# Fifty extra matrix products of ones on TensorE during the weight decode of an attention and SoLU kernel

## The chip, the cores and the metric

The kernel runs on one core of a Trainium2 chip. The metric is the device time of one execution in microseconds; several executions of the same program are timed and their median is given. In the profile PE is TensorE, PEld its weight loads, DVE is VectorE, ACT is ScalarE, POOL is GpSimd and SP is SyncE, which issues most of the DMA transfers; a queue of an engine is written ACTq or SPq.

## What is computed

The reference does two things in a row. For 8 batches and 8 heads of 576 positions with 64 features it computes masked attention (heads 0 to 3 see the last 32 positions, heads 4 to 7 the earlier positions of the same residue modulo 32). The result, 4608 tokens of 512 features, then goes through a feed-forward part with two weight matrices:

```python
scores = np.where(masks, q @ k.T / sqrt(D), -1e9)
attn = softmax(scores); x = attn @ v            # (4608, 512)
h = x @ w_in                                    # w_in (512, 1024)
solu = h * softmax(h)
ln = (solu - mu) / np.sqrt(var + 1e-06) * g_ln
out = ln @ w_out                                # w_out (1024, 512)
```

## The kernel before

The inputs w_in and w_out lie in memory as 64-bit words (double precision), which no engine computes with. So the start of the kernel decodes them: four loads of 1 MB each for w_in (in `prep_w`) and four for w_out (in `prep_o`), issued by SyncE. For each load `decode` has two passes of ScalarE (L619, L620) and one of VectorE (L621) that turn the word into a single-precision number. Of the decoded weights `gram` (L314) forms products of each piece with itself on TensorE, whose diagonal VectorE sums (L318), and `pow2_scale` (L334 on TensorE, L338 and L341 on VectorE) makes a power of two from the sum, by which the weights are scaled. Then w_in is split into a 16-bit high part (L637, ScalarE) and a low part: for two of the four pieces on VectorE (L639), for the other two on TensorE (L647 and L648, with the matrix wdiag from L634) with a copy by ScalarE (L651). The products go to the PSUM tile h_ps, which has three banks. For w_out, L659 to L665 make the scale.

The attention runs beside it in units of up to 12 blocks: scores on TensorE (L439 adds the mask, L444 multiplies q and k, into s_ps), maximum and subtraction on VectorE (L450, L451), exponential on ScalarE (L452), sum and reciprocal on VectorE (L453, L457, L458), scaling on GpSimd (L461), the two 16-bit parts of the weights on ScalarE (L466) and, in the first batches, GpSimd (L468), a transposing DMA by SyncE (L472), the product with v on TensorE (L493, into x_ps), and the split of the result on ScalarE (L509) and VectorE (L510). L381 and L382 on VectorE combine the scales of v and w_in. When the tokens of a tile are there, the feed-forward part follows in 36 tiles of 128 tokens: 24 products with w_in (L551 to L553, into h_ps), row statistics on VectorE (L558 and later), and 24 products with w_out (L594 to L596).

No scheduler orders this. `Plan.add` numbers the steps in the order of the code and notes which step reads or writes what; the list ORDER, written out in the file, gives the sequence in which the steps are emitted, and each engine runs its own steps in that sequence and waits only on the steps it depends on. Steps 36 and following are those of `prep_w` behind the four decodes. The tile `ones` (128 by 128, 16-bit) is filled at the start by VectorE and serves as stationary matrix in L334.

Of the kernel before, what the change touches and what calls it, by code (L numbers as in the profile page):

```python
# [21 lines left out]
P = 128  # L22
# [28 lines left out]
WLO = (0, 1)  # L51


ORDER = [
# [45 lines left out]
]  # L100

BANKED = ("h", "x")
# [59 lines left out]
def attn_solu_kernel(ctx: ExitStack, tc: tile.TileContext, qloc, qstr, kloc, kstr, vloc, vstr, w_in, w_out, g, masks, out):  # L162
    nc = tc.nc
# [79 lines left out]
    add = plan.add  # L243
# [531 lines left out]
```

## Time and profile before

| | |
|---|---|
| median of 3 runs | 503.44 us (501.87 to 504.1) |
| the profiled execution | 503.95 us, span 502.2 us |
| busy: PE | 470.0 us (94%), 4834 products |
| busy: DVE, ACT, POOL | 353.5 us (70%), 292.7 us (58%), 159.6 us (32%) |
| mean granted TensorE clock | 0.979 |
| chain that ended last | PE 81%, DMA 7%, DVE 6%, issue 2%, ACT 2% |

The span is the time from the first to the last instruction of one profiled execution; the execution's own time is a little longer. Busy shares are averages over the whole span, and this kernel has a start of some 60 us, with loads and decoding, that is unlike the rest; so the table tells little about the start, and the views by stretch of time tell more. A busy time of PE counts a product from its start to its modelled end, so that the products of a dense row overlap in it: the distance from start to start is what a product costs there.

### The profile page before, as it was taken

To read this page: it belongs to the slowest core of one execution; us is meant where nothing else is said; L and a number is where in the kernel's file an instruction comes from. 1 tells how busy PE (TensorE), PEld (TensorE's weight loads), DVE (VectorE), ACT (ScalarE), POOL (GpSimd) and SP (SyncE) were. 2 spreads that over 40 slices of the span, in tenths; PEclk is the share of its full clock that TensorE was granted. 3 is DMA by queue.
4 is the path that set the end of the run, shared out by engine and by line. 5 is a ranking of instruction groups with operands and counts; after the bars stand their busy time and mean duration, and the time that the engine had idled before them with its cause. 6 is when DMAs were issued, how large, how long until landed. Compare 5 with 4: busy or idle time off the path is not lost.

```text
span 502.2 us, 11705 instructions
## 1 busy us (share of the span) xinstructions
PE 470.0 (94%) x4834; PEld 246.3 (49%) x4834; DVE 353.5 (70%) x636; ACT 292.7 (58%) x396; POOL 159.6 (32%) x256
## 2 busy tenths in 40 slices
PE   1468799999999999999999999999999999999997
PEld 1455454455445554455445554555445555544443
DVE  2789999688743897498856987488755997665430
ACT  1798886757546556554657365644647554554441
POOL 3324424723160334212331535312510435251120
PEclk9867999999999999999999999999999999999999
DMA  8999998577999499968994997998975789543272
GB/s 248 405 337 297 298 181 197 182 190 110 205 210 264 126 197 240 210 192 167 236 199 138 204 210 199 210 258 152 226 164 160 167 171 183 109 85 82 56 144 77
DMA packets 168102, 96.51 MB, mean 192 GB/s; under 512 B 137840, under 2 KB 154608, under 8 KB 167536
## 3 DMA queue, kind: packets, MB, share of 16 engines
q1 hardware_dynamic: 162432, 84.77, 76.6%
q10 hardware_dynamic: 5616, 10.98, 6.7%
q8 instruction: 38, 0.62, 0.5%
q14 instruction: 16, 0.13, 0.1%
HBM read 40.03 MB, written 9.44 MB: 98 GB/s over the span
## 4 chain that ended last, share of the span: by engine, by line
PE 81%; DMA 7%; DVE 6%; issue 2%; ACT 2%; SPq 1%; POOL 1%; ACTq 0%; DVEq 0%; POOLq 0%
PE h_ps L551 12%; PE h_ps L553 11%; PE h_ps L552 11%; PE o_ps L594 11%; PE o_ps L595 10%; PE o_ps L596 10%; PE x_ps L493 5%; PE s_ps L444 5%; DMA vtwo<-vstr 2%; DMA pt<-p 2%; DMA ct<-c 1%; PE s_ps L439 1%; DMA vrl<-vloc 1%; DVE st L558 1%; DVE obuf L621 1%
## 5 line engine op out<-in xcount | busy, mean ns | idle before, releaser
L461 POOL TENSOR_TENSOR t<-t,m 128x648 f32<-128x648 f32 (+4 forms) x34 | 51.8, 1526 | 201.8 <-DVE m L458 163.6
L551 PE MATMUL h_ps<-w,xhi 128*128 128x512 f16 x280 | 106.3, 380 | 0.8 <-DVE eu L572 0.8
L553 PE MATMUL h_ps<-w,xlo 128*128 128x512 f16 x280 | 106.1, 379 | 0.0
L552 PE MATMUL h_ps<-w,xhi 128*128 128x512 f16 x280 | 106.1, 379 | 0.0
L594 PE MATMUL o_ps<-obuf,ct 128*128 128x512 f16 x272 | 103.3, 380 | 0.5 <-DMA ct<-c 0.3
L596 PE MATMUL o_ps<-obuf,ct 128*128 128x512 f16 x272 | 103.1, 379 | 0.0
L595 PE MATMUL o_ps<-obuf,ct 128*128 128x512 f16 x272 | 103.1, 379 | 0.0
L558 DVE TENSOR_REDUCE st<-h_ps 128x1 f32<-128x1024 f32 x35 | 42.6, 1218 | 36.7 <-PE h_ps L553 36.5
L569 ACT ACTIVATE eu<-h_ps,st,vsc 128x1024 f32<-128x1024 f32 x31 | 37.2, 1201 | 35.8 <-DVE st L559 25.2
L576 ACT ACTIVATE c<-eu,st 128x1024 f16<-128x1024 f32 x36 | 41.2, 1144 | 23.0 <-DVE st L575 18.7
L577 DVE SCALAR_TENSOR_TENSOR c<-eu,st,c 128x1024 f16<-128x1024 f32 x36 | 45.7, 1273 | 11.7 <-ACT c L576 11.6
L572 DVE SCALAR_TENSOR_TENSOR eu<-h_ps,st,eu 128x1024 f32<-128x1024 f32 x35 | 44.7, 1277 | 11.7 <-ACT eu L569 10.8
L444 PE MATMUL s_ps<-k,q 64*54 64x54 f32 (+1 forms) x1280 | 40.5, 273 | 7.9 <-DMA k<-kloc 5.4
L452 ACT ACTIVATE t<-t 128x648 f32<-128x648 f32 (+4 forms) x34 | 26.1, 771 | 35.4 <-DVE t L451 35.0
L579 ACT ACTIVATE junk<-eu,st 128x1024 bf16<-128x1024 f32 x36 | 41.2, 1143 | 7.8 <-DVE st L575 4.7
L551 PEld LDWEIGHTS <-xhi 128*128 128x128 f16 x288 | 28.1, 98 | 35.3 <-issue 1.9
L596 PEld LDWEIGHTS <-ct 128*128 128x128 f16 x288 | 28.2, 98 | 34.0
L553 PEld LDWEIGHTS <-xlo 128*128 128x128 f16 x288 | 28.2, 98 | 34.0
L594 PEld LDWEIGHTS <-ct 128*128 128x128 f16 x288 | 28.1, 98 | 32.7 <-DMA ct<-c 0.7
L444 PEld LDWEIGHTS s_ps<-k,q 64*54 64x54 f32 (+1 forms) x1280 | 39.7, 199 | 8.4 <-DMA k<-kloc 5.6
L585 POOL TENSOR_SCALAR st<-st 128x1 f32<-128x1 f32 x36 | 19.4, 540 | 75.5 <-ACT junk L579 73.4
L552 PEld LDWEIGHTS <-xhi 128*128 128x128 f16 x288 | 28.2, 98 | 31.0
(156 smaller groups left out, 691.2 us busy)
## 6 DMA issues: line engine op xcount, KB each, us to landing
out<-ob ACTq DMA_DIRECT2D x36, 256.0 KB, 3.5
vtwo<-vstr SPq DMA_DIRECT2D x8, 768.0 KB, 7.8
vd<-vtwo SPq DMA_DIRECT2D x14, 384.0 KB, 5.4
vrl<-vloc SPq DMA_DIRECT2D x8, 640.0 KB, 5.2
k<-kstr SPq DMA_DIRECT2D x8, 594.0 KB, 5.4
q<-qloc SPq DMA_DIRECT2D x8, 576.0 KB, 5.7
k<-kloc SPq DMA_DIRECT2D x8, 576.0 KB, 5.4
q<-qstr SPq DMA_DIRECT2D x7, 594.0 KB, 7.4
```

The source lines that it names most:

```text
L444: nc.tensor.matmul(s_ps[row : row + nq, pair, i * nk : (i + 1) * nk], q_raw[half][hs, q0 : q0 + (nq - 1) * nqb + 1 : nqb], k_raw[half][hs, ...
L461: add("pool", lambda: nc.gpsimd.tensor_tensor(tv, tv, sm.unsqueeze(2).broadcast_to([P, nx, nk]), op=ALU.mult), r=TM, w=T)
L551: nc.tensor.matmul(hv[:, i], xhi[:, cc, tok], whi[:, cc, cols], start=(cc == 0), stop=False)
L552: nc.tensor.matmul(hv[:, i], xhi[:, cc, tok], wlo[:, cc, cols], start=False, stop=False)
L553: nc.tensor.matmul(hv[:, i], xlo[:, cc, tok], whi[:, cc, cols], start=False, stop=(cc == 3))
L558: add("dve", lambda: nc.vector.tensor_reduce(low, hv, axis=AX.XY, op=ALU.max, negate=True), r=HH, w=[(ST, "low")])
L572: add("dve", lambda: nc.vector.scalar_tensor_tensor(uv, hv, ia, ev, op0=ALU.mult, op1=ALU.mult, accum_out=us), r=[*HH, E, (ST, "ia")], w=[ ...
L576: add("act", lambda: nc.scalar.activation(c[:, 0], u, AF.Identity, bias=mean, scale=1.0), r=[U, (ST, "mean")], w=[(C, 0)])
L577: add("dve", lambda: nc.vector.scalar_tensor_tensor(c[:, 1], u, mean, c[:, 0], op0=ALU.add, op1=ALU.subtract), r=[U, (ST, "mean"), (C, 0)] ...
L594: nc.tensor.matmul(o, ct[:, cc, :], ohi[:, cc, :], start=(cc == 0), stop=False)
L595: nc.tensor.matmul(o, ct[:, cc, :], olo[:, cc, :], start=False, stop=False)
L596: nc.tensor.matmul(o, ct[:, 8 + cc, :], ohi[:, cc, :], start=False, stop=(cc == 7))
```

## The change

Fifty steps are added to `prep_w` behind the decodes. Each is one product on TensorE: the stationary matrix is `ones`, the moving one is `ones` too, repeated four times to 512 columns, and the result goes to the third bank of h_ps. Nothing reads it before the bank is written anew. In the list ORDER the new steps are 36 to 85, all later numbers grow by 50, and the fifty are put in at eight places. Apart from that the sequence is the old one, and the programs of VectorE, ScalarE, GpSimd and SyncE are the same. The places, in the order of time on TensorE: two behind the L314 products of v and ahead of the first L334; eighteen behind that L334; thirteen behind the L314 products of the first piece of w_in; one between those of the third and the fourth piece; four behind the fourth; two between the L334 of w_in and that of v; two behind the latter; eight ahead of the unit whose masks are added at 39.33 us. The diff, with the list cut to one line:

```diff
 WLO = (0, 1)
+WARM = 50
...
-    12, 1, 2, 11, 9, 10, 15, 14, 16, 20, 3, 17, 24, 7, 18, 0, 13, 4, 8, 28, 5, 32, 70, 71, 72, 83, 73, 74, 84, 75, 85, 76, 59, 86, 77, 78, 60, 79, 21, 61, 87,
+    12, 1, 2, 11, 9, 10, 15, 14, 16, 20, 3, 17, 24, 7, 18, 0, 13, 4, 8, 28, 5, 32, 120, 121, 122, 133, 123, 124, 134, 125, 135, 126, 109, 136, 127, 128, 110,
+    129, 21, 111, 137, 36, 37, 112, 113, 114, 22, 138, 139, 146, 23, 118, 147, 116, 38, 39, 40, 41, 42, 43, 44, 45, 46, 47, 48, 49, 50, 51, 52, 53, 54, 55,
...
             decode(stage[cc], w_in[cc * P : (cc + 1) * P].rearrange("p (c f t) -> p c f t", c=2, t=2), ST[cc], ROOMS[cc], cc)
 
+        def idle():
+            nc.tensor.matmul(h_ps[:, 2], ones, ones.unsqueeze(1).broadcast_to([P, 4, P]), start=True, stop=True)
+
+        for _ in range(WARM):
+            add("pe", idle, r=["ones"], w=[("h", 2)])
         gram(w_sc[:, 4:5], [(flat[cc], ST[cc]) for cc in range(4)], "wm", (h_ps[:, 0, 0:P], ("h", 0)), (ob_sb[1][:, 0 : P // 2].bitcast(BF16), ("ob", 1)))
```

In the rows below, a line number of the changed kernel is 3 larger than that of the kernel before up to the new code, and 8 larger behind it; L636 is the new product. A row names the operation, the tile it writes, the tiles it reads and the shape.

On TensorE, before, the two L334 products (the scales of w_in and of v) are followed by the masks of the next unit:

```order
L334 LDWEIGHTS ones_110
L334 MATMUL h_ps<-w_sc_115,ones_110 128x1
L334 LDWEIGHTS ones_110
L334 MATMUL s_ps<-vs_78,ones_110 128x1
L439 LDWEIGHTS unit_85
L439 MATMUL s_ps<-mk_loc_83,unit_85 64x288
```

In the changed kernel, at the same place:

```order
L337 LDWEIGHTS ones_110
L337 MATMUL h_ps<-w_sc_115,ones_110 128x1
L636 LDWEIGHTS ones_110
L636 MATMUL h_ps<-ones_110 128x512
L636 LDWEIGHTS ones_110
L636 MATMUL h_ps<-ones_110 128x512
L337 LDWEIGHTS ones_110
L337 MATMUL s_ps<-vs_78,ones_110 128x1
```

Two of the new products now stand between the two scales (and two more behind the second).

On TensorE, before, the scores of one unit (k and q of the near positions, x12 instructions in a row) are followed at once by the masks of the unit that starts at 39.33 us:

```order
L439 LDWEIGHTS unit_85
L439 MATMUL s_ps<-mk_loc_83,unit_85 64x288
L444 MATMUL s_ps<-k_65,q_63 64x96 x12
L439 LDWEIGHTS unit_85
L439 MATMUL s_ps<-mk_str_84,unit_85 64x324
```

In the changed kernel the new products follow those scores:

```order
L442 LDWEIGHTS unit_85
L442 MATMUL s_ps<-mk_loc_83,unit_85 64x288
L447 MATMUL s_ps<-k_65,q_63 64x96 x12
L636 LDWEIGHTS ones_110
L636 MATMUL h_ps<-ones_110 128x512
```

Eight such pairs stand there before the masks follow.

## Rows read from the trace of the kernel before

**Rows 1.** The page's second part: the span in 40 equal slices of 12.56 us; each digit is a busy share in tenths, PEclk the granted TensorE clock in tenths.
```profile
PE   1468799999999999999999999999999999999997
...
PEclk9867999999999999999999999999999999999999
```

**Rows 2.** The windows view: the stretch (us from the span's start) and its length, then the busy time, with the number of instructions, of PE, PEld, DVE, ACT and POOL, then the granted clock, the DMA share and GB/s. The first four cover the two stretches at the lower clock, the one between them, and the time from the chain's last VectorE link to the end; the last is VectorE's run up to that link.
```profile
20.70:34.40 13.70, 7.88 (x132) 6.66 (x132) 13.19 (x14) 13.17 (x15) 2.36 (x3) 0.50 1.10 363
34.40:37.80 3.40, 1.32 (x30) 1.03 (x31) 2.41 (x12) 3.40 (x6) 1.74 (x6) 1.00 1.00 351
37.80:44.60 6.80, 5.27 (x94) 3.27 (x95) 6.28 (x15) 5.79 (x7) 2.81 (x3) 0.50 1.17 258
62.40:502.20 439.80, 433.14 (x4231) 219.85 (x4230) 306.89 (x548) 247.94 (x344) 136.97 (x214) 1.00 0.81 174
45.60:62.30 16.70, 14.00 (x209) 8.62 (x208) 16.23 (x29) 15.11 (x20) 7.10 (x6) 1.00 1.09 322
```

**Rows 3.** The chain of waits in order of time, three of its pieces between 57 and 63 us: start, length, engine and line.
```profile
60.50 0.18 DVE m L457
...
61.11 1.23 DVE o_sc L665
...
62.39 0.16 PE o_ps L334
```

**Rows 4.** The timeline of PE between 18 and 45 us: start, busy time, line, operation, and in brackets the idle time before it and what ended that.
```profile
18.30 0.16 PE L334 MATMUL o_ps<-vm,ones 128*128 128x1 bf16 x1 [0.47 <-DVE junk L318]
...
24.13 1.25 PE L444 MATMUL s_ps<-k,q 64*64 64x96 f32 x24 [5.42 <-DMA k<-kloc]
...
28.26 0.45 PE L439 MATMUL s_ps<-mk_loc,unit 64*64 64x288 bf16 x4 [1.91 <-DVE t L451]
...
32.00 1.92 PE L314 MATMUL h_ps<-ct 128*128 128x128 bf16 x16
34.83 0.18 PE L334 MATMUL h_ps<-w_sc,ones 128*128 128x1 bf16 x1 [0.91 <-DVE ob L318]
...
36.41 0.32 PE L439 MATMUL s_ps<-mk_loc,unit 64*64 64x288 bf16 x4 [0.34 <-DVE vsc L338]
36.53 0.86 PE L444 MATMUL s_ps<-k,q 64*64 64x96 f32 x24
39.33 0.49 PE L439 MATMUL s_ps<-mk_str,unit 64*64 64x324 bf16 x4 [1.94 <-DVE vsc L341]
...
40.96 0.27 PE L659 MATMUL o_ps<-unit,gm 128*1 128x128 bf16 x1
41.16 2.08 PE L647 MATMUL h_ps<-c,wdiag 128*128 128x512 f32 x2
...
43.59 1.24 PE L493 MATMUL x_ps<-pt,vd 118*64 118x54 f16 x40
```

**Rows 5.** The timeline of PE later, at the granted clock 1.00: the same products as some of group 4, and two products of 512 columns in a row.
```profile
45.93 1.02 PE L647 MATMUL h_ps<-c,wdiag 128*128 128x512 f32 x2
...
47.10 0.28 PE L493 MATMUL x_ps<-pt,ve 96*64 96x64 f16 x6
...
71.98 0.94 PE L493 MATMUL x_ps<-pt,vd 118*64 118x54 f16 x48
...
104.81 0.33 PE L439 MATMUL s_ps<-mk_str,unit 64*64 64x324 bf16 x4
...
106.26 0.39 PE L594 MATMUL o_ps<-obuf,ct 128*128 128x512 f16 x1
106.49 0.38 PE L595 MATMUL o_ps<-obuf,ct 128*128 128x512 f16 x1
```

**Rows 6.** The timeline of DVE between 33 and 58 us.
```profile
33.05 0.72 DVE L450 TENSOR_REDUCE m<-s_ps 128x6 f32<-128x576 f32 x1
...
41.26 0.28 DVE L660 TENSOR_REDUCE gm<-o_ps 1x1 f32<-1x128 f32 x1 [0.35 <-PE o_ps L659]
...
45.58 0.72 DVE L510 TENSOR_TENSOR xlo<-x_ps,xhi 128x540 f16<-128x540 f32 x1 [0.16 <-ACT xhi L509]
...
48.06 0.28 DVE L382 TENSOR_SCALAR vsc<-consts,vsc,w_sc 128x2 f32<-128x2 f32 x1
...
49.88 0.45 DVE L457 TENSOR_SCALAR m<-m 128x12 f32<-128x12 f32 x1
...
51.70 1.11 DVE L382 TENSOR_SCALAR vsc<-consts,vsc,w_sc 128x2 f32<-128x2 f32 x1
...
57.78 1.23 DVE L621 SCALAR_TENSOR_TENSOR obuf<-obuf,eu 128x1024 int32<-128x1024 int32 x1
```

**Rows 7.** The timeline of ACT between 43 and 57 us.
```profile
43.70 0.59 ACT L651 CAST w<-h_ps 128x512 f16<-128x512 f32 x1 [0.69 <-PE h_ps L648]
44.94 0.61 ACT L509 CAST xhi<-x_ps 128x540 f16<-128x540 f32 x1 [0.66 <-PE x_ps L493]
...
55.28 1.16 ACT L619 ACTIVATE obuf<-eu 128x1024 f32<-128x1024 f32 x1 [0.16 <-DMA eu<-w_out]
56.34 1.24 ACT L620 ACTIVATE eu<-eu,consts 128x1024 int32<-128x1024 uint32 x1
```

**Rows 8.** The timeline of POOL between 49 and 53 us.
```profile
49.01 1.29 POOL L468 TENSOR_TENSOR p<-t,p 128x576 f16<-128x576 f32 x1 [3.00 <-ACT p L466]
50.67 2.12 POOL L461 TENSOR_TENSOR t<-t,m 128x648 f32<-128x648 f32 x1 [0.37 <-DVE m L458]
```

89 rows, old and new, of the table ORDER are left out of this document.

## The prediction

> **What bounds the kernel now.** I read the 40 slices of the page first. TensorE is filled from about the fifth slice on and has holes before; its granted clock is below full only in the slices ahead of that [rows 1]. The stretches show where: the clock stands at 0.50, which is 1.2 GHz, from about 20.8 to 34.4 us and from 37.8 to 44.6 us, and at 1.00, 2.4 GHz, between them and for all the rest [rows 2]. From 62.4 us to the end TensorE is busy 433.14 of 439.80 us at 1.00: there it is the bound, nothing of its clock is left to win, and whatever ends the first 62 us sooner moves the end by as much. So the whole question is what sets the 62.4 us.
>
> The chain of waits answers it: the last link before TensorE's unbroken work is VectorE's L665 at 61.11, on which TensorE's L334 at 62.39 waits [rows 3]. Behind it VectorE has been at work almost without a stop: 16.23 of the 16.70 us from 45.6 to 62.3, while in the first cold stretch it was busy 13.19 of 13.70 us and ScalarE 13.17 [rows 2]. TensorE was busy 7.88 us there. The start is thus paced by VectorE and ScalarE and, behind them, by the loads; TensorE's low clock counts only where one of those two stands still for it. The reader should look for such places, and there are four: VectorE idles 0.35 us before L660 at 41.26 and 0.16 us before L510 at 45.58 (this one through ScalarE) [rows 6]; ScalarE idles 0.69 us before L651 at 43.70 and 0.66 us before L509 at 44.94 [rows 7]. All four lie at the end of the second cold stretch.
>
> **The fifty products.** Each has 512 columns and 128 rows; at 1.00 two like it start 0.23 us apart (106.26, 106.49) [rows 5]. At 0.50 I price one by the 16 products of 128 columns that take 1.92 us at 32.00: four of them are 0.48 us [rows 4]. They have no inputs to wait for, and every other engine's program is unchanged, so they cost only where TensorE comes late to its next real product. Gap by gap, at 1.00:
> Two stand ahead of L334 at 18.30, which had 0.47 us of waiting: 0.46 us, covered. Eighteen follow: 4.1 us from 18.46, to 22.6, and the masks behind them; the next real product waits for a load until 24.13 after 5.42 us of idleness. Covered, with about 1 us over.
> Thirteen stand ahead of L439 at 28.26, whose wait was 1.91 us: they need 3.0 us. But the neighbours shrink if the clock holds: the 24 products of L444 from 1.25 to 0.86 us (24.13 against 36.53), the eight of L314 by a quarter of 1.92, that is 0.48. The wait then has 2.8 us, TensorE is 0.2 late, and the scores from there are first read by VectorE at 33.05 [rows 4, 6]: covered.
> One and four stand within and behind L314 at 32.00, 1.15 us; the wait before L334 at 34.83 was 0.91 and the 16 products give back up to 0.96. Four lie between 35.01 and 36.41: 0.92 us in 1.40, less 0.16 for the L334 between them. Covered, within 0.1 to 0.2 us.
> Eight stand ahead of L439 at 39.33: 1.84 us in a wait of 1.94. This is the tightest place: cover 0.1 us. At 0.50 they take 3.84, and TensorE is late by 1.9 [rows 4].
>
> **What the clock gives back.** Before the clock fell at about 20.8 and 37.8 TensorE had been mostly idle (1.32 us of work in the 3.40 us to 37.8), and it rose at 44.6 after a stretch in which TensorE had 5.27 us of work in 6.80 [rows 2]. With the products in the waits it has work through nearly all of 17.8 to 45 us, so I take it to stay at 1.00 from 37.8 to 44.6. Then:
> VectorE. L439 and L444 at 39.33 take 1.63 us to L659; the same two take 1.45 at 104.81 to 106.26. L659 takes 0.27, and half of it is 0.13. L660 comes 0.18 to 0.31 sooner of its 0.35 [rows 4 to 6]. The 0.16 at 45.58 goes too. Together 0.34 to 0.47; I take 0.4. No clock can give VectorE more than the whole 0.51.
> ScalarE. From L647 to the start of L493 takes 2.43 us (41.16 to 43.59) and 1.17 at 1.00 (45.93 to 47.10); forty products of L493 take 1.24 and at 1.00 40/48 of 0.94, 0.78 [rows 4, 5]. TensorE then ends this work more than 1.6 us sooner, and both waits of ScalarE go: 1.35 us.
>
> **Where that goes.** ScalarE's gain ends at 55.28: there it already waits 0.16 us for the last load of the output weights [rows 7]. That load stands in SyncE's queue behind transposes which by the program follow ScalarE and GpSimd, and ScalarE first waits for TensorE at 43.70; so I take its landing as fixed. ScalarE's second decode step ends at 56.34 + 1.24 = 57.58 as before, and VectorE's L621, which reads it, started at 57.78 [rows 6]. So VectorE may come to this place as early as it likes; it gains at most 0.20 us beyond it. The cover of TensorE's low clock is this load and these two engines.
> Something can also be lost on the way. L382 on VectorE takes 0.28 us at 48.06 but 1.11 at 51.70, where it ends at 52.81, just when GpSimd's L461 (50.67 + 2.12 = 52.79) does: it stood still for it [rows 6, 8]. GpSimd's L468 at 49.01 waits for ScalarE; 1.35 sooner is 47.66, and the first L382, 0.4 sooner, is at 47.66 too. If it falls behind L468 it loses 0.83. In return L457 at 49.88 is free of L468, 0.45 to 0.18 [rows 3, 6], 0.27 back. So VectorE arrives at L621 between 0.4 + 0.27 = 0.67 early, cut to 0.20 by the load, and 0.4 - 0.83 + 0.27 = -0.16, late. I take a gain of 0.1, nearer the early end, since L382 is caught only if L468 starts first, and the two start together.
>
> **The sum.** The profiled execution took 503.95 us, the median of the three runs is 503.44, 0.51 below. 503.95 - 0.1 = 503.85 for a like execution, 503.3 for the median. Within 0.5% (2.5 us) counts as no change, about what a measurement of this kernel can tell; the runs of the one kernel before spread from 501.87 to 504.10.
>
> **The rivals.**
> (a) The products do not hold the clock: it falls as before. Where they stay covered the time is that of before, 503.4. For it: TensorE still idles from about 22.9 to 24.1.
> (b) The load is no fixed end, or lands sooner. Then VectorE's own count holds, 0.51 of idle time and the 0.27 of L457, 0.8 us at most: 502.6. Against it: the 0.16 us idle before 55.28 ends with that load.
> (c) Slower: the eight products ahead of L439 at 39.33 run at 0.50. They end 1.9 us late, L659 and with it VectorE's L660 come 1.9 later, and VectorE, with next to no idle time from there to 62.3, passes it to the end: 505.2. It decides from the point at which they take longer than 1.94 us, 0.24 each. For it: in the trace the clock fell at 37.8, in just this place. Against it: eight more products stand in the 4 us ahead.
> (d) TensorE's cold work paces the start after all, in one place or another of the two stretches at 0.50. It is 7.88 + 5.27 = 13.15 us [rows 2]; the full clock gives back half of it, 6.6 us: 496.8. Against it: VectorE was busy 13.19 of the 13.70 us of the first stretch, and of TensorE's gain only the four idle places above can pass on.
> The Trainium skill (TensorE: Matmul & The Clock Gate, Terms) goes further than (d): it puts the penalty of a throttled clock at the throttled time times one minus the clock's share. By the page's rule, as an estimate, the 20.5 us of the two stretches would be worth some 10 us, an end near 493. The trace does not bear it out, since in those stretches TensorE itself had only 13.15 us of work.
>
> **How the numbers follow.** Forecast 0.55; (a) 0.13; (b) 0.14; (c) 0.12; (d) 0.03; 0.03 for what I do not see, such as several groups running at 0.50 and pushing the 33.05 reader. The range reaches from (b) with the spread of the runs, 501.9, to (c), 505.3. Forecast, (a), (b) and (c) all lie within 2.5 us of before: same 0.86, with the tails of (b) and (d) faster 0.07, the tails of (c) slower 0.07.
>
> **What would show it.** Right: granted clock 1.00 through 20.8 to 45 us, L647 at about 41 in half its time, no idle time before L651 and L509, more idle time on ScalarE before the last load of the output weights, and L665 ending within a few tenths of 62.3. Wrong: L439 at 39.33 late, a landing of that load at another time, or a difference that arises after 62.4, where I expect a plain shift.

## The result, and the profile after

The changed kernel takes 507.15 us (median of 20 runs, 503.97 to 510.43) beside 503.45 us (20 runs, 501.39 to 506.65) of the kernel before on the same chip. The ratio is 1.0074, with a 95% interval of 1.0052 to 1.0096: 3.7 us slower. The prediction, 503.3 us with no change, was wrong, and the time lies above its range.

The profiled execution of the changed kernel is one of its quicker ones, 504.28 us with a span of 502.6 us. It shows most of what was forecast and, beside it, two things that were not. The windows view first (columns as in [rows 2], the first three and the last being the stretches shown there, the fourth a new one):

```profile
20.70:34.40 13.70, 11.22 (x164) 6.82 (x163) 13.19 (x15) 12.42 (x13) 2.62 (x3) 1.00 1.09 356
34.40:37.80 3.40, 1.53 (x26) 0.71 (x27) 1.18 (x6) 2.85 (x5) 1.19 (x5) 1.00 1.03 375
37.80:44.60 6.80, 6.58 (x125) 4.15 (x118) 6.49 (x15) 6.80 (x8) 2.81 (x3) 1.00 1.28 217
62.60:66.10 3.50, 3.42 (x10) 1.19 (x10) 3.26 (x10) 2.05 (x3) 1.06 (x2) 0.51 1.27 146
62.40:502.60 440.20, 434.64 (x4231) 220.33 (x4230) 307.15 (x549) 247.97 (x344) 137.24 (x215) 1.00 0.81 174
```

The clock stands at 1.00 through both stretches that were at 0.50. VectorE was busy 13.19 us of the first before and is so now: it gained nothing there. In the second stretch it is busy 1.18 us where it was 2.41. And there is a new stretch at 0.50, from 62.60 to 66.10 us, in TensorE's unbroken work.

The timeline of PE (columns as in [rows 4]):

```profile
22.26 0.32 PE L442 MATMUL s_ps<-mk_loc,unit 64*64 64x288 bf16 x4
...
27.95 0.32 PE L442 MATMUL s_ps<-mk_loc,unit 64*64 64x288 bf16 x4
...
36.76 0.16 PE L337 MATMUL s_ps<-vs,ones 128*128 128x1 bf16 x1 [1.87 <-DVE w_sc L341]
...
38.22 1.90 PE L636 MATMUL h_ps<-ones 128*128 128x512 bf16 x8
40.19 0.33 PE L442 MATMUL s_ps<-mk_str,unit 64*64 64x324 bf16 x4
...
41.69 0.22 PE L667 MATMUL o_ps<-unit,gm 128*1 128x128 bf16 x1
41.84 1.12 PE L655 MATMUL h_ps<-c,wdiag 128*128 128x512 f32 x2
```

The scale of v (36.76) was at 35.90 before: it comes 0.86 us late, behind a wait of 1.87 us. The eight products take 1.90 us, and the masks behind them stand at 40.19, not 39.33. The timelines of ACT and of DVE say why the scale is late. First the rows of before, of PE and of ACT:

```profile
35.90 0.16 PE L334 MATMUL s_ps<-vs,ones 128*128 128x1 bf16 x1 [0.90 <-DVE vs L327]
...
34.09 1.48 ACT L375 ACTIVATE junk<-vtwo 128x1536 bf16<-128x1536 f32 x1
```

Then those of the changed kernel, of ACT and of DVE:

```profile
34.95 1.48 ACT L378 ACTIVATE junk<-vtwo 128x1536 bf16<-128x1536 f32 x1 [1.47 <-DMA vtwo<-vstr]
...
43.77 0.56 ACT L659 CAST w<-h_ps 128x512 f16<-128x512 f32 x1
44.26 0.61 ACT L512 CAST xhi<-x_ps 128x540 f16<-128x540 f32 x1
...
55.59 1.15 ACT L622 ACTIVATE obuf<-eu 128x1024 f32<-128x1024 f32 x1 [0.24 <-DMA eu<-w_out]
```

```profile
36.55 0.16 DVE L330 TENSOR_REDUCE vs<-vm 128x1 bf16<-128x2 f32 x1 [2.35 <-ACT junk L378]
...
41.95 0.28 DVE L668 TENSOR_REDUCE gm<-o_ps 1x1 f32<-1x128 f32 x1 [0.17 <-PE o_ps L667]
...
48.50 1.12 DVE L385 TENSOR_SCALAR vsc<-consts,vsc,w_sc 128x2 f32<-128x2 f32 x1
...
61.74 0.88 DVE L673 TENSOR_TENSOR o_sc<-gm 128x1 f32<-128x1 f32 x1
```

TensorE is not the cause. ScalarE squares a part of the second batch's v (L378, the tile vtwo) and waits 1.47 us for its load, where before it came to these squares without a wait, just after the load had landed (34.04 us); VectorE (L330, then L341) waits 2.35 us for ScalarE; TensorE waits for VectorE. ScalarE's two waits of [rows 7] before L659 and L512 are gone, and it waits 0.24 us before 55.59. The chain of waits (start, length, engine and tile) names the load, and behind 62.68 the products at half clock:

```profile
26.47 8.40 DMA vtwo<-vstr
...
62.68 0.16 PE o_ps L337
62.84 0.45 PE h_ps L554
...
66.24 0.22 PE h_ps L556
```

The load was issued at 26.47 us. Before, it was issued at 27.04 and took 7.0 us; now it comes sooner, takes 8.4 and lands 0.8 us later. The DMA view of before at the load's issue:

```profile
vtwo<-vstr SPq DMA_DIRECT2D x1, 768.0 KB, 7.0
```

The DMA view of the changed kernel (queue, packets, MB, share of 16 engines; then an issue with its KB and us to landing), of 31 to 34.9 us and of the load's issue:

```profile
q8 instruction: 1, 0.02, 1.8%
...
vtwo<-vstr SPq DMA_DIRECT2D x1, 768.0 KB, 8.4
```

Between 31 and 34.9 us one packet of 16 KB goes through the queue that the view names instruction; 1.8% of 16 engines for 3.9 us are 1.1 us on one. In this execution all this costs little: the product that waits for o_sc is at 62.68, not 62.39 [rows 3], 0.29 later. From there the new stretch at 0.50 gives TensorE 1.50 us more busy time (434.64 against 433.14, [rows 2]); less idle time in the rest takes up most of it, and the span grows by 0.4 us in all. The median execution loses 3.7, so the rest had to be looked for in other executions: each lists its mean granted clock, and of the 20 the three quickest stand at 0.997 to 0.998 (504.0 to 505.1 us), two at 0.996 (505.7 and 506.0), the others at 0.989 to 0.993 (506.6 to 510.4).

### The profile page after: what moved, and what is told of

Read it like the earlier page. It is cut to its first block, busy times and chain, and to the rows that moved or that the text cites. A ratio compares the mean times of both kernels' runs of the same rounds, so it can differ in the third digit from the quotient of the medians.

```text
span 502.6 us, 11805 instructions
## 1 busy us (share of the span) xinstructions
PE 478.6 (95%) x4884; PEld 248.6 (49%) x4884; DVE 353.3 (70%) x636; ACT 292.7 (58%) x396; POOL 159.9 (32%) x256
## 4 chain that ended last, share of the span: by engine, by line
PE 84%; DVE 8%; DMA 4%; issue 2%; ACT 1%; POOL 0%; ACTq 0%; DVEq 0%; POOLq 0%
PE h_ps L554 12%; PE h_ps L555 12%; PE o_ps L597 12%; PE h_ps L556 12%; PE o_ps L599 11%; PE o_ps L598 11%; PE s_ps L447 6%; PE x_ps L496 5%; DMA vtwo<-vstr 4%; PE s_ps L442 2%; DVE obuf L624 1%; PE o_ps L317 1%; DVE st L561 1%; PE s_ps L599 1%; DVE vd L397 1%
## 5 line engine op out<-in xcount | busy, mean ns | idle before, releaser
L455 ACT ACTIVATE t<-t 128x648 f32<-128x648 f32 (+4 forms) x34 | 26.1, 770 | 35.3 <-DVE t L454 34.9
L599 PEld LDWEIGHTS <-ct 128*128 128x128 f16 x288 | 28.2, 98 | 34.0
L597 PEld LDWEIGHTS <-ct 128*128 128x128 f16 x288 | 28.1, 98 | 32.2
L598 PEld LDWEIGHTS <-ct 128*128 128x128 f16 x288 | 28.2, 98 | 31.1
```

The source lines that it names most:

```text
L597: nc.tensor.matmul(o, ct[:, cc, :], ohi[:, cc, :], start=(cc == 0), stop=False)
L598: nc.tensor.matmul(o, ct[:, cc, :], olo[:, cc, :], start=False, stop=False)
L599: nc.tensor.matmul(o, ct[:, 8 + cc, :], ohi[:, cc, :], start=False, stop=(cc == 7))
```

## The experiments

In every kernel below each product of the reference's computation is still there; only products that nobody reads come and go. The fifty stay at their eight places unless said. The kernel before was timed along with each set on the same chip: 503.64, 503.22, 502.97 and 503.14 us for the four sets in their order below. A loss in us is the ratio less one, times 503; the distance of two medians can differ from it by some tenths, and for the second sample of the changed kernel by 1.1 us (2.5 by the ratio, 3.6 by the medians).

**Is it the clock alone?** The first theory was that the clock falls in TensorE's last waits ahead of 62 us. Four kernels ran together. The changed kernel and the kernel before, unchanged, are a second sample of each:

> The changed kernel once more, unaltered, for the granted clock of each execution beside its time. T1 (the clock falls in TensorE's last waits ahead of its unbroken work, so that the first products there run at 0.50; the first profile showed it from 62.6 to 66.1 us): the mean granted clock differs between executions and the span follows it, about 1.7 us more for each 0.0034 of mean clock; a second profile shows a stretch at 0.50 near or behind 62 us, and none or little of it elsewhere. T2 (no clock in it: the fifty products come late to the real ones, and VectorE hands the lateness on): span and mean clock are unrelated, and L337 behind o_sc starts 3 us or more after the 62.4 us of the kernel before. T3 (the clock falls somewhere in the dense part behind 70 us): the stretch at 0.50 is there.

> The kernel before, unaltered, as the counterpart: all three theories give ratio 1.000 within its interval. T1: a mean clock of about 0.979 in most executions, which is the 20 us at 0.50 in the first 45 us, and seldom less; a stretch at 0.50 near 62 us is rare here. If falls near 62 us are as frequent here as in the changed kernel, T1 does not explain the difference.

The other two put eleven more products into the last two waits:

```diff
+        def fill():
+            nc.tensor.matmul(h_ps[:, 2], ones, ones.unsqueeze(1).broadcast_to([P, 4, P]), start=True, stop=True)
+        for _ in range(11):
+            add("pe", fill, r=["ones"], w=[("h", 2)])
```

In the list five stand ahead of the products x_ps of one unit and six ahead of the L337 product of o_sc, once in the changed kernel and once in the kernel before.

> The changed kernel with eleven more products of ones: five in TensorE's wait of 1.25 us ahead of the x_ps products at 57.06, six in the wait of 1.44 us ahead of the o_sc product at 62.68. T1: the clock no longer falls there, the mean clock is 0.998 or more in nearly all executions, and the time is 3 to 4 us below the changed kernel, 502.5 to 504. T2: the eleven cost what they are late, time 507 or a little above. T3: as the changed kernel, 507.

> The kernel before with the same eleven products in the same two waits and none of the fifty. T1: if the kernel before sometimes loses the clock there too, the time falls by up to 1 us and the spread shrinks to the lower end, 501.5 to 503; the mean clock stays 0.979 for the first 45 us. T2 and T3: no change, 503.4.

Measured: the changed kernel again 507.27 us, ratio 1.0050 (1.0019 to 1.0080); the kernel before again 503.07, 0.9992 (0.9972 to 1.0012); the changed one filled 506.46, 1.0052 (1.0027 to 1.0077); the one before filled 504.77, 1.0026 (0.9998 to 1.0054).

The second sample shows the clock's part. Its four executions at a mean clock of 0.999 to 1.000 took 502.6 to 504.1 us, as the kernel before; seven at 0.990 to 0.993 took 507.0 to 509.7. Its profiled execution is of the latter kind. Windows view, then the timeline of PE:

```profile
38.20:41.60 3.40, 3.40 (x20) 1.12 (x12) 3.30 (x8) 3.40 (x4) 1.38 (x2) 0.50 1.20 183
65.50:68.90 3.40, 3.40 (x10) 1.17 (x10) 3.16 (x9) 2.06 (x3) 0.00 (x0) 0.50 1.14 242
```

```profile
36.92 0.16 PE L337 MATMUL s_ps<-vs,ones 128*128 128x1 bf16 x1 [1.81 <-DVE vs L330]
...
38.46 3.45 PE L636 MATMUL h_ps<-ones 128*128 128x512 bf16 x8
41.84 0.33 PE L442 MATMUL s_ps<-mk_str,unit 64*64 64x324 bf16 x4
...
43.28 0.22 PE L667 MATMUL o_ps<-unit,gm 128*1 128x128 bf16 x1
...
65.47 0.16 PE L337 MATMUL o_ps<-o_sc,ones 128*128 128x1 bf16 x1 [2.58 <-DVE o_sc L673]
```

Here the clock falls behind the wait of 1.81 us, exactly onto the eight: 3.45 us in place of 1.90. L667 comes at 43.28, 1.59 us later than in the execution above and 2.32 later than before; o_sc's product comes at 65.47, 3.08 later than before. VectorE adds to it on the way: from the last L624 to L673 it takes 4.36 us where it took 3.33, and one L460 of 1.21 us in place of 0.17 makes that difference.

But the clock in the last waits is not the main cause. The filled kernel kept a mean clock of 0.996 to 1.000 in ten of its 12 executions and was as slow as the second sample of the changed one; in its profile the clock fell elsewhere, once at the very place where the load is late and once far behind, from 217.5 us:

```profile
36.60:40.00 3.40, 3.01 (x33) 1.53 (x33) 2.61 (x9) 3.40 (x7) 2.25 (x5) 0.50 1.58 354
217.50:220.90 3.40, 3.15 (x42) 2.10 (x42) 2.46 (x7) 2.32 (x3) 0.00 (x0) 0.50 0.06 23
```

Such a late fall does not need the fifty products: the profile of the kernel before, run again, has one from 212.9 to 216.3 us.

The filled kernel before settles nothing; its interval reaches to no change. So the load came under suspicion. The DMA view of the kernel before, run again (of 32.7 to 35 us, and of the load's issue):

```profile
q8 instruction: 1, 0.02, 2.9%
...
vtwo<-vstr SPq DMA_DIRECT2D x1, 768.0 KB, 7.0
```

Its load was issued at 25.71 and took 7.0 us, to 32.7; the packet came at 33.2, after it.

**Is it the instruction packet?** The theory now: TensorE's program has 100 more instructions (each product loads its stationary matrix first), so the packet that fetches the next block is asked for earlier and falls into the load. Four kernels ran together. The first has the fifty with one row and one column, which add the instructions but hardly any work:

```diff
-            nc.tensor.matmul(h_ps[:, 2], ones, ones.unsqueeze(1).broadcast_to([P, 4, P]), start=True, stop=True)
+            nc.tensor.matmul(h_ps[0:1, 2, 0:1], ones[:, 0:1], ones[:, 0:1], start=True, stop=True)
```

The second has only the last sixteen, with 4, 2, 2 and 8 at the last four of the eight places:

```diff
-        for _ in range(WARM):
+        for _ in range(16):
```

The third has 94 such tiny products (`short`) ahead of all others of TensorE. They are 188 instructions, and with the 68 of the first four places 256, 16 KB, ahead of the place where the packet is asked for:

```diff
-        for _ in range(WARM):
-            add("pe", idle, r=["ones"], w=[("h", 2)])
+        for i in range(144):
+            add("pe", short if i < 94 else idle, r=["ones"], w=[("h", 2)])
```

The fourth fills the wait for the scale of v, with nine full products ahead of it in place of two:

```diff
-        for _ in range(WARM):
+        for _ in range(57):
```

> The fifty products at their places, but each with one column and one row of the array in use, so that TensorE's program is as long as in the changed kernel (7232 rows) and the work and the clock are nearly those of before. T5 (code loading: TensorE's longer program brings a 16 KB packet of the instruction queue, which is at 34.3, 33.2 and 34.0 us in the three profiles without the fifty, to 31.8 to 32.0 us in the three with them, in the middle of the vtwo load, which then lands 8.4 us after its issue and not 7.0; ScalarE's squares wait for it, and all behind comes about 1 us late): the vtwo load takes 8.4 us again, the product o_ps<-o_sc starts about 1 us later than before, time 504 to 505. T1 (the clock's falls alone, which the warm products bring about): load 7.0 us, time as before, 503.5.

> Only the last sixteen of the fifty (four, two, two and eight), behind the place where the packet of code falls; the first thirty-four are left out. T5: the packet stays near 34 us, the vtwo load takes 7.0 us, the time is that of before or up to 0.5 us less, 503 to 503.5. T1: the wait ahead of 62 us is unchanged and the late part is as in the changed kernel: 505 to 507.

> The changed kernel with 94 tiny products (one row, one column) ahead of TensorE's first product, so that up to the packet's place the program is longer by 34 + 94 = 128 products, 256 instructions or 16 KB, and the next packets fall where they fell before. T5: the vtwo load takes 7.0 us again, and what is left is the changed kernel without the late load: 503 to 504.5, with the clock's falls rarer. T1 and T2: no better than the changed kernel, 507.

> The changed kernel with seven more products in the wait that the late load makes longer (1.87 us ahead of the product s_ps<-vs at 36.8). T5 with the clock as its second part (in this wait the clock falls in some executions, and then the eight products ahead of 40 us run at 0.50 and cost 1 to 1.4 us more): the load stays late, 8.4 us, but the clock holds to 55 us, time 504.5 to 506, that is 1 to 2 us below the changed kernel. If the falls near 62 us make most of the loss: 507 as the changed kernel.

Measured: fifty tiny 504.27 us, 1.0028 (1.0012 to 1.0044); last sixteen 504.65, 1.0023 (1.0004 to 1.0043); realigned 504.22, 1.0031 (1.0011 to 1.0050); filled wait 507.24, 1.0079 (1.0060 to 1.0099).

The fifty tiny leave TensorE's clock cold in the start, as before (0.50 from 21.6 to 45.5 us), and still lose 1.4 us. Their profile also has a fall at 62.6 us, which the profiles of the kernel before lack; but executions at a like mean clock, 0.978 to 0.983, show the loss too: 503.4 to 505.8 us with a median of 503.9 in five, beside a median of 503.0 in 16 of the kernel before. ACT's timeline and the DMA view (31 to 34.9 us, and the issue) show the same late load:

```profile
34.72 1.48 ACT L377 ACTIVATE junk<-vtwo 128x1536 bf16<-128x1536 f32 x1 [1.50 <-DMA vtwo<-vstr]
```

```profile
q8 instruction: 1, 0.02, 1.7%
...
vtwo<-vstr SPq DMA_DIRECT2D x1, 768.0 KB, 8.5
```

With the program realigned, the packet is at 33.71 and the load takes 6.6 us (DMA view, 33 to 34 us and the issue); the scale of v is at 35.54. Of the 3.7 us the fifty then cost 1.6. In its profile the clock falls once, at the end of the start (windows view):

```profile
q8 instruction: 1, 0.02, 7.0%
...
vtwo<-vstr SPq DMA_DIRECT2D x1, 768.0 KB, 6.6
```

```profile
58.50:61.90 3.40, 3.40 (x52) 3.20 (x49) 3.26 (x11) 2.82 (x6) 2.27 (x2) 0.50 1.17 253
```

The last sixteen keep the packet behind the load too (34.14, 7.0 us), yet at 504.65 they take more than expected: in the profile the last w_out load takes 11.5 us (10.3 before) and the clock falls at 58.94, but the product that waits for o_sc stands at 62.38, as before, so what they lose there comes behind it. The filled wait holds the clock from 17.3 to 215.2 us and gains nothing. The fourteen added instructions bring the next packet to 41.89 us, into the transpose of the second pt (DMA view, around the packet and at the transpose's issue):

```profile
q8 instruction: 1, 0.02, 24.5%
...
pt<-p SPq DMA_TRANSPOSE x1, 9.7
```

It takes 9.7 us where the changed kernel has 8.3 and the one before 7.0. The load `room` behind it in SyncE's queue is issued at 45.03, not 43.28, and o_sc's product stands at 63.05. The expectation was missed. The packet in the transpose can be part of the reason, but o_sc's product is only 0.66 us later than before; 2.3 us more than before pass behind it, where the clock falls at 215.2 us, and what makes them wasn't tested.

**Which work costs the rest?** In one kernel the last eight of the changed kernel are tiny:

```diff
-            add("pe", idle, r=["ones"], w=[("h", 2)])
+            add("pe", idle if i < 42 else short, r=["ones"], w=[("h", 2)])
```

In the other the fifty are replaced by twelve products in single precision, 5, 3, 1, 1 and 2 of them at five of the places, so that 12 steps stand in the code rather than 50:

```diff
+    (ones32,) = buf("ones32", [P, P])
...
-            nc.tensor.matmul(h_ps[:, 2], ones, ones.unsqueeze(1).broadcast_to([P, 4, P]), start=True, stop=True)
+            nc.tensor.matmul(h_ps[:, 2], ones32, ones32.unsqueeze(1).broadcast_to([P, 4, P]), start=True, stop=True)
...
-        for _ in range(WARM):
+        for _ in range(12):
```

> The changed kernel, in which only the last group, the eight products ahead of the masks at 39 us, has one row and one column; the length of TensorE's program and all other groups are unchanged. T5 with the clock as its second part (the late load lengthens TensorE's wait ahead of 36.8 us, the clock falls there in some executions, and the eight products at 0.50 come late): the load still takes 8.4 us and s_ps<-vs starts near 36.8, but o_ps<-unit,gm follows it by 5.0 us and not by up to 6.4, whatever the clock does; time 504.5 to 505.5, near that of the fifty tiny products. If the falls near 62 us make most of what is left: 507.

> Instead of the fifty, twelve products of a single-precision matrix of ones with 512 columns (five, three, one, one and two at the places of the groups of eighteen, thirteen, one, two and eight), which take about 0.86 us each at full clock: the same work for TensorE with far fewer instructions. T5: the packet of code falls at 33 us or later, the vtwo load takes 7.0 to 7.3 us, the clock holds through the start, and the time is that of before within 0.5%, 502.5 to 504. T1: as the changed kernel, 506 to 507.

Measured: last eight tiny 504.88 us, 1.0026 (1.0007 to 1.0045); twelve in single precision 509.27, 1.0097 (1.0062 to 1.0132). In the first the load is late (8.5 us) and the clock falls behind it, here for twice as long, windows view and timeline of PE:

```profile
37.20:44.00 6.80, 5.38 (x93) 3.72 (x92) 6.02 (x16) 6.78 (x7) 2.89 (x6) 0.50 1.25 213
```

```profile
36.88 0.16 PE L336 MATMUL s_ps<-vs,ones 128*128 128x1 bf16 x1 [1.83 <-DVE vs L329]
...
38.95 0.34 PE L635 MATMUL h_ps<-ones 128*1 128x1 bf16 x8
...
42.33 0.27 PE L669 MATMUL o_ps<-unit,gm 128*1 128x128 bf16 x1
```

Late load, fallen clock, and yet only 1.3 us: the eight take 0.34 us, and a wait of 1.42 us is left before the masks. Without eight full products at half clock the loss goes from 3.7 to 1.3. The twelve did not do what they were made for: their packet still falls at 32.79 us, inside the load (8.6 us). They are also more instructions than was meant. The timeline shows each as two products, the first five as ten:

```profile
17.63 4.54 PE L638 MATMUL h_ps<-ones 128*128 128x512 f32 x10
```

The page lists 4858 products and 4858 weight loads where it lists 4834 of each before, so the twelve add 48 rows, and the fifty 100. The packet's time lies between those with the fifty and those of before, and whether the count alone sets it or also how early TensorE comes through the code was not tested. Why they are the slowest of all stays open; three executions at a mean clock of 0.998 to 1.000 took 504.3 to 505.1 us, six at 0.989 to 0.993 took 508.4 to 511.1.

**Put together, and the code alone.** One kernel has both edits shown above, that of the realigned and the eleven of the filled one. The other is the kernel before with nothing but 128 tiny products, 256 instructions, ahead of all others:

```diff
+        for _ in range(128):
+            add("pe", idle, r=["ones"], w=[("h", 2)])
```

Here `idle` is the product with one row and one column.

> The realigned changed kernel (94 tiny products ahead of all others) with the eleven more products of ones in the waits ahead of 57 and 62 us. If what the realigned kernel still loses on the kernel before comes from the clock's falls between 58 and 66 us: mean clock 0.998 or more in nearly all executions and 502.5 to 503.5. If it comes from elsewhere: 504 or more, as without the eleven.

> The kernel before with 128 tiny products (one row, one column) ahead of all others and none of the fifty: TensorE's program is longer by just 256 instructions, 16 KB, so the packets of code fall where they fell, with one more near 13 us. T5: the vtwo load takes 7.0 us or less, the clock and the time are those of before, 503.0 to 503.6, although more instructions were added than the fifty bring. If added code costs in itself, wherever its packets fall: 504.5 or more.

Measured: realigned and filled 504.71 us, 1.0019 (0.9997 to 1.0041), above what was expected, though not to be told from the kernel before; code alone 503.15, 1.0006 (0.9990 to 1.0022), as expected. So more instructions cost nothing in themselves that could be measured; the interval leaves room for 1.1 us. In the code's profile one more packet passes at 7.5 us and the next ones lie as before, 34.09 with a load of 5.7 us. No kernel tried beats the one before.

The packets and the load in all 14 profiles, in the order of the packet's time (us; landing is issue plus duration):

| kernel | packet | load lands | load takes |
|---|---|---|---|
| fifty tiny | 31.34 | 34.64 | 8.5 |
| changed, filled | 31.81 | 35.12 | 8.5 |
| changed | 31.83 | 34.87 | 8.4 |
| filled wait | 31.92 | 34.89 | 8.4 |
| last eight tiny | 31.93 | 35.00 | 8.5 |
| changed again | 32.00 | 34.97 | 8.4 |
| twelve in single precision | 32.79 | 35.03 | 8.6 |
| before again | 33.20 | 32.71 | 7.0 |
| realigned | 33.71 | 33.34 | 6.6 |
| before, filled | 33.95 | 33.65 | 7.0 |
| realigned and filled | 34.06 | 33.71 | 6.8 |
| code alone | 34.09 | 33.32 | 5.7 |
| last sixteen | 34.14 | 33.85 | 7.0 |
| before | 34.34 | 34.04 | 7.0 |

Seven packets fall inside the load, and those loads take 8.4 to 8.6 us; seven fall 0.3 to 0.8 us after its landing, and those take 5.7 to 7.0.

What this does to the end of the start can be read from the product that waits for o_sc, in the same profiles. With the load in time it stands at 60.35 to 62.39 us in four (before; before again; before, filled; code alone) and at 62.07 to 62.38 in the other three. With the load late it stands at 62.68 to 63.05 in five, in which the clock held there or no eight full products of the fifty stood behind the wait, and at 65.47 and 65.66 in the two where the clock falls behind the wait and the eight full products follow (changed again; changed, filled).

The executions of the realigned kernel, sorted by mean clock, show that what it still loses goes with the falls of the clock: six at 0.999 to 1.000 took 503.1 to 504.6 us with a median of 503.5, near the 503.2 of the kernel before, and six at 0.993 to 0.997 took 503.4 to 507.2 with a median of 506.0. Of the realigned and filled kernel nine at 0.999 to 1.000 have a median of 503.5. That is a sorting and no experiment: no run changes the clock alone.

## Why the prediction was wrong, point by point

**Right.** That VectorE, ScalarE and the loads pace the start: the clock was held through it, and neither VectorE's busy time nor o_sc moved forward. That the groups of two, eighteen and thirteen are covered: the real products behind the latter two stand at 22.26 and 27.95. That ScalarE's two waits go and the last load of the weights takes up the gain: both seen. That L385 can be caught by GpSimd: it takes 1.12 us at 48.50, as priced. Where the clock holds throughout, the kernel takes about the time forecast, 502.6 to 504.1 us in four executions of the second sample; no profile shows what the load did in them.

**The steps that failed** are two. The first is "every other engine's program is unchanged, so they cost only where TensorE comes late to its next real product". The new instructions also have to be loaded, by DMA, while the kernel's data is. This term was missing from the sum. Alone, without work on TensorE, it measured 1.4 us (fifty tiny, 0.6 to 2.2 by the interval); 256 instructions, a whole packet, cost nothing that could be measured (code alone). The landings of the loads were thus not given, though the prediction took that of the last weights as fixed by its queue: ScalarE's step behind it starts at 55.59, not 55.28.

The second is "so I take it to stay at 1.00 from 37.8 to 44.6". It held there in the changed kernel's first profile, but fell from 38.2 to 41.6 us in the second, where the eight then took 3.45 us and o_sc's product came 3.08 us late. This is the larger part of the loss, as far as the runs tell: with the eight tiny 1.3 us are left of the 3.7, though the load is late and the clock falls. Of the first 20 executions 15 stand at a mean clock of 0.993 or lower, as that one does; where it fell in them is not recorded.

The Trainium skill (Runtime: NRT & Kernel Launch, Instruction fetch mechanics) says that instructions are refilled in blocks of 16 KiB, 256 of them, over a DMA queue of the sequencer, and that crossing a boundary costs one DMA tail-bump, mostly hidden. The trace agrees on the block: shifting by 256 instructions brought the packet back behind the load. On the price it agrees where the packet passes outside the load (code alone, 1.0006), and not where it falls inside: there the load took 1.4 us longer, and the kernel with it 1.4 us (fifty tiny).

**Rival (c) had the mechanism and was given too little chance.** It said 505.2 us, the eight running at 0.50 in 3.84 us and 1.9 us late; in the second sample's profile they take 3.45 us and delay L667 by 2.32, of which the load has its 0.86 to 1.02. Its price was too low all the same, since VectorE does not hand on the 2.32 but adds to it, and o_sc's product comes 3.08 late. Its condition was misjudged: "eight more products stand in the 4 us ahead" counts the work and not the wait. The load lengthened that wait to 1.8 us and more, with nothing to do in it, and there the clock fell, in some executions and not in others. That the eight make most of the loss beyond the load was tested (last eight tiny, where the clock falls and 1.3 us are lost).

**"Nothing of its clock is left to win" after 62.4, and a plain shift.** TensorE's clock could be lost there. Behind its last wait it ran at 0.50 from 62.66 to 66.07, and a product took 0.43 us rather than 0.22: eight of them, 1.7 us. The Trainium skill (TensorE: Matmul & The Clock Gate, Terms) prices this as throttled time times one minus the clock's share, 3.4 times 0.5 here, and on the engine that bounds the kernel the row agrees. In this execution little of it reached the end, in the second sample's 1.1 us more than before passed between o_sc's product and the end (440.9 against 439.8). In the four profiles with a fall between 159 and 221 us 441.8 to 442.9 us pass there, 438.8 to 441.2 in the other ten; and one of the four is the kernel before, run again. The prediction had no rival of this kind.

**Of the sum**, 3.7 us: the load by itself 1.4 us (fifty tiny); most of the rest comes where the late load, the fallen clock and the eight meet, since to take away the load's lateness (realigned, 1.6 left) or the eight (1.3 left) takes away over 2 us each. Measured against the second sample of the changed kernel (1.0050) it is about 1 us each, and the intervals overlap, so the shares are rough. The parts do not add up as separate terms. What the late load costs the changed kernel when its clock holds isn't measured: the 1.4 us are those of a kernel whose clock is cold in the start.

**Open.** Why the realigned kernel keeps 1.6 us: its executions with the clock held lose next to nothing, but the kernel that fills the waits at 57 and 62 us as well can't be told from either side, and its profile lost the clock at 159.5 us instead. Why the clock falls in some executions of one program and not in others. Why the twelve lose most. How one packet of 1.1 us on one engine makes the load 1.4 us longer; that the load's share on that engine lands last is an inference. The packet's record names no engine; that it is TensorE's rests on its program being the only one that changed, on moving it, and on the count, 38 such packets in the profile of the kernel before and 39 in each of the three kernels with tiny products ahead of all others.

## What to carry to other kernels

Work that costs an idle engine nothing still has code, and the code is loaded by the DMA engines at moments that shift with the instructions added: look where the instruction queue's packets fall among the loads on the chain, before and after. Try such a change also as its code alone (the products cut to one row) and its code moved by a whole packet, to separate the two costs. Products put in to hold the clock and placed behind a long wait run at half clock when it falls in that wait, and turn from cover into delay. To put them into the wait is not enough: the one kernel that did so (filled wait) held its clock there and gained nothing.

## What the runs showed of the hardware that was not expected

- One 16 KB packet of the instruction queue inside a 768 KB load: 8.4 to 8.6 us for the load in seven profiles; behind it 5.7 to 7.0 in seven. Inside a transpose, in one profile: 9.7 us against 8.3 and 7.0.
- 256 added instructions in front of everything: 503.15 us, ratio 1.0006 (0.9990 to 1.0022).
- The granted clock fell in executions of one and the same program at different places and not in all of them: mean clocks from 0.990 to 1.000, times from 502.6 to 509.7 us.
